# A linear-attention block and a ReLU block: contiguous loads of x, 70 small warming matmuls, the keys' weight on ScalarE's queue, and a new written order

## The chip, the cores and the metric

The kernel runs on 1 core of one Trainium2 chip. The metric is the device time of one execution in microseconds (us), the median of several runs. A core has five engines that work side by side, each on its own list of instructions in order: TensorE (matmuls and weight loads), VectorE, ScalarE, GpSimd and SyncE, which here only issues DMAs. They wait for each other by semaphores.

## The reference

The input x has S = 2048 rows of D = 512 numbers in bfloat16; H = 32 heads of 16; Dff = 1792.

```python
def _A_ref(x, wqkv, wo):          # x is already layer-normed
    qkv = (x @ wqkv) ...          # q, k, v: heads of 16
    phi = lambda t: jnp.where(t > 0, t + 1, jnp.exp(t)) + 1e-6
    pq, pk = phi(q), phi(k)
    kv = jnp.einsum("bhsd,bhse->bhde", pk, v)
    z = jnp.einsum("bhsd->bhd", pk)
    num = jnp.einsum("bhqd,bhde->bhqe", pq, kv)
    den = jnp.einsum("bhqd,bhd->bhq", pq, z)[..., None] + 1e-6
    return (num / den) ... @ wo
def _B_ref(x, w1, w2):
    return relu(x @ w1) @ w2
h = x + _A_ref(_layernorm(x), A_wqkv, A_wo)
return h + _B_ref(_layernorm(h), B_w1, B_w2)
```

The sums over all rows (kv and z) have to be finished before the first row of the attention's output can be made.

## The kernel before

x lies in 16 tiles of 128 rows. Before, row 16 p + t is row p of tile t (`x_v`), so that one tile's rows lie 16 KB apart in memory; the output uses the same order (`of_v`). Tiles are grouped in four chunks of four, 512 columns once they are transposed.

The order of all work is written out by hand in the string `ORDER`. A word such as `K.4.0` calls `op_K(4, 0)`. The words are gone through once, and each engine gets its instructions in the order in which the words issue them; only data, the reuse of a buffer and the reuse of one of eight DMA semaphores make an engine wait. Moving a word past words of other engines alone changes nothing.

First phase, per tile t of x: `lx` loads (SyncE), `S` and `A` make the statistics (VectorE), `R` makes the reciprocal deviation in two small steps (ScalarE), `N` normalises (VectorE; with two more numbers, some of the four 128-column blocks). The normalised tile is then transposed into `lnT`: tiles 0 to 5 by `T` on TensorE, four 128-column matmuls, and a copy out of PSUM by `E` (ScalarE) or `V` (VectorE); tiles 6 to 15 by a DMA transpose, `X`. `K` multiplies a tile's `lnT` by the keys' weight wk (four 512-column matmuls); phi is made of `F` and `U` (ScalarE: exp and relu) and `M` and `D` (VectorE); `G` adds the tile's share of the 512 x 512 product of normalised x and phi(k) to four PSUM banks (four matmuls, bank 4 to 7). After the last tile, `z` sums phi(k) over the rows, `gA`/`gD` copy G out, and `kv`, `kx`, `m` make one matrix of wv and wo that stands for the attention. `Q`, `qF`, `qU`, `qM`, `qD` make phi(q), chunk by chunk.

Second phase, per chunk: `d4`, `dl4`, `dx4` make the reciprocal of den. It is spread over the partitions by `rp` and `rm` for chunk 0 and by a round through memory (`wb`, eight `rb`, `dm`) for the others. Per tile `h` (four matmuls) and `hD` give h; `s`, `a`, `n`, `r` are its layer norm; `t` with `e`/`v` (chunk 0) or `x` (a DMA transpose, chunks 1 to 3) transpose it. `p` is one 128-column block of the product with w1 (four matmuls), `pA`/`pD` its ReLU out of PSUM, `f` the product with w2 (14 matmuls a tile), `fo` the last addition, `fd` the store of a tile. PSUM has eight banks; the last index of `K`, `Q`, `p` and others names the bank.

`lk`, `lq`, `lv`, `lo`, `l1`, `l2` load the weights, all from SyncE. `warm` runs matmuls on zeros, with no reader.

Of the kernel before, what the change touches and what calls it, by code (L numbers as in the profile page):

```python
# [15 lines left out]


ORDER = """
table const masks warm.9.7 lx.1.1 S.1 lx.0.1 S.0 A.0 A.1 lx.2.2 R.1.1 R.0.1 S.3 S.2 A.3 A.2 N.0.0.2 N.0.2.2
N.1 lk.0.2 lx.4.2 lk.2.2 lx.6.2 T.0.0.0.2 warm.1.7 T.0.3.2.2 T.1.1 R.2.2 N.2 T.2.2 E.0.0.2 E.0.2.2 K.0.0 N.3  # L20
S.4 S.5 A.4 A.5 T.3.3 E.1 E.2 F.0.1 K.1.1 U.0.1 R.4.2 F.1.1 V.3 U.1.1 K.3.3 K.2.2 S.6 M.0.1 S.7 D.0.1 N.4 A.6
A.7 M.1.1 N.5 G.0 T.4.0 lo.2.2 lx.8.4 lx.12.4 D.1.1 T.5.1 G.1 R.6.2 F.2.1 E.4 E.5 U.2.1 N.6 S.9 S.8 M.2.1 N.7
A.9 A.8 D.2.1 F.3.1 R.8.2 U.3.1 S.11 M.3.1 X.6 K.4.0 K.5.1 X.7 F.4.2 U.4.2 N.9 D.3.1 S.10 M.4.2 N.8 A.11 D.4.2
A.10 R.10.2 G.2 K.6.2 G.3 K.7.3 F.6.2 U.6.2 S.12 S.13 N.10 A.12 N.11 M.6.2 A.13 X.9 X.8 lq.0.2 lq.2.2 X.10
X.11 D.6.2 R.12.2 G.4 G.5 K.9.1 K.8.0 F.8.2 U.8.2 G.6 G.7 K.10.2 K.11.3 F.10.2 S.14 N.12 N.13 M.8.2 A.14 S.15
D.8.2 A.15 M.10.2 U.10.2 R.14.2 D.10.2 N.14 N.15 X.12 G.8 K.12.0 X.13 X.14 X.15 lv.0.2 l1.0.2 lo.0.2 lv.2.2
l2.0.7 l1.2.2 l2.7.7 K.13.1 U.12.2 F.12.2 M.12.2 G.9 G.10 G.11 Q.0.1.1 Q.0.0.0 K.14.2 K.15.3 qF.0.0.2 qU.0.0.2
F.14.2 U.14.2 D.12.2 G.12 Q.0.3.1 Q.0.2.0 G.13 qM.0.0.2 qD.0.0.2 M.14.2 D.14.2 G.14 z.3.2 z.0.2 z.1.2 z.2.2
qF.0.2.2 qM.0.2.2 zc G.15 gD.0.2 qU.0.2.2 gA.2.2 qD.0.2.2 Q.1.1.3 Q.1.0.2 qU.1.0.2 qF.1.0.2 kv.3.4 kv.0.4
kv.1.4 kv.2.4 kx zh Q.1.3.1 m.0.4 m.1.5 d4.0.3 m.2.6 m.3.7 Q.1.2.0 mD.0.2 dl4.0 dx4.0 qF.1.2.2 qU.1.2.2  # L30
Q.2.1.3 mD.2.2 qM.1.0.2 rp.0.0.4 rp.0.3.7 rp.0.2.6 rp.0.1.5 qM.1.2.2 rm.0.0.2 rm.0.2.2 qD.1.2.2 qD.1.0.2
Q.2.0.2 Q.2.3.1 Q.2.2.0 h.0.4 h.2.6 h.3.7 h.1.5 hD.0 s.0 a.0 n.0 t.0.4 qU.2.0.2 qF.2.0.2 qU.2.2.2 qF.2.2.2 e.0
Q.3.0.2 d4.1.4 hD.2 hD.1 s.2 s.1 hD.3 a.1 a.2 s.3 n.2 a.3 n.1 n.3 Q.3.1.3 Q.3.2.0 Q.3.3.1 t.2.6 t.1.5 t.3.7
dl4.1 dx4.1 qF.3.0.2 qU.3.0.2 e.2 v.1 v.3 wb.1 p.0.0.2 p.0.1.3 rb.1.4 rb.1.2 rb.1.6 rb.1.0 rb.1.5 rb.1.3
rb.1.1 rb.1.7 qF.3.2.2 pD.0.0.2 qU.3.2.2 p.0.2.0 p.0.3.1 p.0.4.2 p.0.5.3 pD.0.4.2 dm.1.0.2 pA.0.2.2 dm.1.2.2
qM.2.2.2 p.0.7.1 p.0.6.0 p.0.8.2 qM.3.2.2 qM.2.0.2 h.7.7 pA.0.6.2 hD.7 h.4.4 hD.4 s.4 qD.3.2.2 h.5.5 h.6.6 a.4
hD.6 hD.5 s.5 s.6 a.6 qM.3.0.2 p.0.11.1 p.0.10.0 a.5 n.6 s.7 qD.2.0.2 a.7 pA.0.10.2 n.4 n.5 p.0.9.3 pA.0.8.2
f.1.5.0.7 p.0.13.3 p.0.12.2 n.7 pA.0.12.2 r.0.4 f.0.4.0.7 f.0.4.7.7 f.3.7.0.7 qD.2.2.2 fo.0 qD.3.0.2 d4.2.4
x.6 x.4 x.5 x.7 f.2.6.0.7 p.1.0.0 p.1.2.2 p.1.3.3 f.3.7.7.7 p.1.1.1 f.1.5.7.7 pD.1.0.2 dl4.2 dx4.2 wb.2 fd.0
rb.2.0 rb.2.4 rb.2.6 rb.2.2 rb.2.1 rb.2.5 rb.2.3 rb.2.7 pA.1.2.2 dm.2.0.2 p.1.6.2 p.1.7.3 dm.2.2.2 pA.1.6.2  # L40
p.1.4.0 p.1.5.1 pA.1.4.2 r.4.4 f.2.6.7.7 fo.3 h.11.7 h.8.4 fo.2 hD.11 fo.1 hD.8 s.11 a.11 s.8 p.1.11.3 p.1.8.0
h.9.5 a.8 hD.9 s.9 a.9 p.1.9.1 h.10.6 hD.10 s.10 a.10 n.8 n.10 p.1.10.2 pD.1.10.2 n.9 pA.1.8.2 p.1.13.1
p.1.12.0 pA.1.12.2 f.4.4.0.7 f.4.4.7.7 n.11 fo.4 fd.1 x.9 fd.3 x.10 x.8 x.11 f.5.5.0.7 d4.3.4 f.7.7.0.7
f.6.6.0.7 f.6.6.7.7 p.2.3.3 dl4.3 r.8.4 dx4.3 p.2.0.0 p.2.2.2 p.2.1.1 f.7.7.7.7 pA.2.0.2 wb.3 rb.3.6 fd.2
rb.3.0 rb.3.4 rb.3.2 rb.3.1 rb.3.5 rb.3.3 rb.3.7 fo.7 fo.6 fd.6 fd.7 p.2.4.0 p.2.5.1 f.5.5.7.7 pA.2.4.2
dm.3.2.2 dm.3.0.2 pA.2.2.2 fo.5 p.2.9.1 h.12.4 h.14.6 h.15.7 h.13.5 p.2.8.0 hD.15 hD.14 hD.12 pA.2.8.2 p.2.7.3
p.2.6.2 p.2.13.1 pA.2.6.2 s.14 hD.13 s.13 a.13 s.12 a.14 s.15 a.15 n.14 a.12 f.8.4.0.7 p.2.10.2 f.9.5.0.7
p.2.11.3 p.2.12.0 n.15 n.12 n.13 pD.2.10.2 f.10.6.0.7 x.13 x.14 x.12 x.15 fd.5 fd.4 r.12.4 pA.2.12.2 f.9.5.7.7
f.10.6.7.7 p.3.1.1 p.3.2.2 p.3.0.0 p.3.3.3 f.8.4.7.7 fo.8 pA.3.0.2 f.11.7.0.7 fo.9 pA.3.2.2 p.3.6.2 p.3.7.3
pA.3.6.2 p.3.5.1 p.3.4.0 p.3.10.2 p.3.11.3 pA.3.4.2 p.3.8.0 p.3.9.1 f.11.7.7.7 pA.3.8.2 fo.11 fo.10 fd.10  # L50
f.12.4.0.7 p.3.13.1 p.3.12.0 f.13.5.0.7 pD.3.10.2 pA.3.12.2 f.15.7.0.14.0.2 f.14.6.0.7 f.13.5.7.7 f.12.4.7.7
fd.11 fd.9 fd.8 fo.13 fo.15.0.2 fo.12 fd.12 fd.15.0.2 fd.13 f.14.6.7.7 fo.14 fd.14 f.15.4.0.14.2.1 fo.15.2.1
fd.15.2.1 f.15.5.0.14.3.1 fo.15.3.1 fd.15.3.1
"""


# [1 line left out]
def kernel(  # L58
# [10 lines left out]
    nc = tc.nc  # L69
    P = 128  # L70
    xf = A_x.flatten_outer_dims()
    of = out.flatten_outer_dims()
    S, D = xf.shape
# [4 lines left out]
    CW = 512  # L78
# [7 lines left out]
    NO = 4  # L86

    const = ctx.enter_context(tc.tile_pool(name="const", bufs=1))
# [3 lines left out]

    ctx.enter_context(tc.manual_schedule())

    x_v = xf.rearrange("(p t) d -> p t d", p=P)
    of_v = of.rearrange("(p t) d -> p t d", p=P)
    wqkv_v = A_wqkv.rearrange("(k p) n -> p k n", p=P)
    wo_v = A_wo.rearrange("(k p) n -> p k n", p=P)
    w1_v = B_w1.rearrange("(k p) n -> p k n", p=P)
# [2 lines left out]
    x_nat = big.tile([P, NT, D], BF16, name="x_nat")  # L102
    wq_sb = const.tile([P, KD, D], BF16, name="wq_sb")
    wk_sb = const.tile([P, KD, D], BF16, name="wk_sb")
# [30 lines left out]
    rb = big.tile([P, NE, 2, CW], BF16, name="rb")  # L135
# [6 lines left out]
    o_t = gT  # L142
    zeros = m_sb[:, 0, :]
    bk = psum.tile([P, 8, CW], F32, name="bk")
# [52 lines left out]


    def op_lx(t, n):
        nc.sync.dma_start(out=x_nat[:, t : t + n, :], in_=x_v[:, t : t + n, :])  # L200

    def load_d(dst, src, k, n):
        nc.sync.dma_start(out=dst[:, k : k + n, :], in_=src[:, k : k + n, :])

    op_lk = lambda k, n: load_d(wk_sb, wqkv_v[:, :, D : 2 * D], k, n)
    op_lq = lambda k, n: load_d(wq_sb, wqkv_v[:, :, 0:D], k, n)
    op_lv = lambda k, n: load_d(wv_sb, wqkv_v[:, :, 2 * D : 3 * D], k, n)
    op_lo = lambda k, n: load_d(wo_sb, wo_v, k, n)
    op_l1 = lambda k, n: load_d(w1_sb, w1_v, k, n)
    op_l2 = lambda k, n: load_d(w2_sb, w2_v, k, n)  # L210

    def op_warm(n, b):
        for _ in range(n):
            nc.tensor.matmul(bk[:, b, :], lhsT=zeros[:, 0:P], rhs=zeros, start=True, stop=True)


    op_S = lambda t: nc.vector.bn_stats(out=st[:, t, :], in_=x_nat[:, t, :])  # L217
# [271 lines left out]

    def op_fd(t, k=0, w=KD):  # L490
        cols = slice(k * P, (k + w) * P)
        nc.sync.dma_start(out=of_v[:, t, cols], in_=o_t[:, t % NO, cols])

    ops = {k[3:]: v for k, v in locals().items() if k.startswith("op_")}
    for word in ORDER.split():
# [32 lines left out]
```

## Time and profile before

| | |
|---|---|
| median of 3 runs | 175.04 us (173.61, 175.04, 175.33) |
| profiled execution | 175.75 us, of which the span is 174.0 us |
| TensorE busy | 165.3 us, 870 matmuls |
| VectorE, ScalarE, GpSimd busy | 90.3, 69.9, 4.7 us |
| first DMA issue | 0.80 us |
| last output issue | 171.62 us |
| HBM read, written | 9.44 MB, 2.49 MB |

The span runs from the first to the last instruction of the profiled execution; the device time of the same execution is 1.75 us longer. A matmul's length in the profile includes its way through the array, so matmuls overlap; what they cost is the distance between their starts. A line of the timeline has start, length, engine, line of the source, operation, out<-in, shape and count, and in brackets the idle time of the engine before it and what ended that. In the profile's DMA lists "to landing" is the time from an issue on SyncE to the arrival of the last of its 16 completions.

### The profile page before, as it was taken

Reading aid. Unit: us, or ns where it says so; the run is one execution under the profiler, and the core shown is the slowest. Engines: PE = TensorE matmul, PEld = TensorE weight load, DVE = VectorE, ACT = ScalarE, POOL = GpSimd, SP = SyncE. Lnnn points to the kernel's source line nnn. Section 1 sums busy time; section 2 is a strip of 40 time slices with the busy share of each in tenths; the row PEclk is TensorE's granted clock in tenths of the full one; section 3 lists DMA queues with packets and bytes.
Section 4 is the critical chain, followed back from the end, with each engine's and each line's share of the span. In section 5 each row is a group of like instructions: output and inputs, shape, how many; then the busy total and the mean of one; then the engine's idle time right before and its main releaser. Section 6 shows DMA issues by size and latency. Waiting matters only on the chain.

```text
span 174.0 us, 2293 instructions
## 1 busy us (share of the span) xinstructions
PE 165.3 (95%) x870; PEld 77.5 (45%) x886; DVE 90.3 (52%) x194; ACT 69.9 (40%) x102; POOL 4.7 (3%) x21
## 2 busy tenths in 40 slices
PE   7499989999999989999999999999999999999993
PEld 2255434446534444444444444444444444444643
DVE  3779975532689935995305597101659201205043
ACT  2488756675678582243321322302414204241100
POOL 7300000000000000000000000000000000000000
PEclk9999999999999999999999999999999999999999
DMA  4951454289900032004131000555200430002104
GB/s 123 317 223 30 90 157 90 49 276 363 375 25 2 0 101 53 0 0 86 38 120 61 0 30 2 122 65 145 66 0 0 90 94 0 0 0 86 34 4 121
DMA packets 22475, 14.97 MB, mean 86 GB/s; under 512 B 13248, under 2 KB 21312, under 8 KB 22464
## 3 DMA queue, kind: packets, MB, share of 16 engines
q1 hardware_dynamic: 22464, 14.82, 29.9%
q8 instruction: 7, 0.11, 0.3%
q14 instruction: 4, 0.03, 0.1%
HBM read 9.44 MB, written 2.49 MB: 69 GB/s over the span
## 4 chain that ended last, share of the span: by engine, by line
PE 85%; DVE 5%; DMA 5%; issue 1%; ACT 1%; SPq 0%
PE bk L448 28%; PE bk L477 28%; PE bk L433 8%; PE bk L287 8%; PE bk L331 5%; PE bk L279 4%; DMA lnT<-h_nat 3%; DMA x_nat<-in_A_x_dram 2%; DVE st L217 2%; PE bk L250 1%; PE bk L339 1%; PE bk L386 1%; PE bk L373 1%; DVE h_nat L231 1%; ACT eb L297 1%
## 5 line engine op out<-in xcount | busy, mean ns | idle before, releaser
L448 PE MATMUL bk<-lnT,w_sb 128*128 128x512 bf16 x223 | 51.1, 379 | 0.8 <-DVE lnT L269 0.7
L477 PE MATMUL bk<-w_sb,at 128*128 128x512 bf16 (+2 forms) x244 | 50.3, 355 | 0.4
L463 ACT ACTIVATE at<-bk 128x1024 bf16<-128x1024 f32 x22 | 22.2, 1023 | 62.0 <-PE bk L448 56.8
L477 PEld LDWEIGHTS <-at 128*128 128x128 bf16 x252 | 23.4, 98 | 25.1 <-issue 0.5
L485 DVE SCALAR_TENSOR_TENSOR gT<-bk,rstd,h_nat 128x512 bf16<-128x512 f32 (+2 forms) x18 | 12.1, 688 | 43.0 <-PE bk L477 42.8
L448 PEld LDWEIGHTS <-w_sb 128*128 128x128 bf16 x224 | 21.8, 98 | 27.3 <-issue 0.9
L297 ACT ACTIVATE eb<-bk 128x1024 bf16<-128x1024 f32 (+1 forms) x18 | 16.7, 927 | 7.2 <-PE bk L279 4.2
L300 ACT ACTIVATE rb<-bk 128x1024 bf16<-128x1024 f32 (+1 forms) x18 | 16.7, 928 | 1.2 <-PE bk L287 1.0
L279 PE MATMUL bk<-wk_sb,lnT 128*128 128x512 bf16 x64 | 16.1, 390 | 0.8 <-DMA lnT<-h_nat 0.7
L287 PE MATMUL bk<-lnT,wq_sb 128*128 128x512 bf16 x62 | 14.9, 379 | 0.2 <-issue 0.2
L433 PE MATMUL bk<-m_sb,pqs 128*128 128x512 bf16 x63 | 14.6, 379 | 0.1
L468 DVE TENSOR_SCALAR at<-bk 128x1024 bf16<-128x1024 f32 x6 | 7.3, 1222 | 13.9 <-PE bk L448 13.9
L331 PE MATMUL bk<-at,h_nat 128*128 128x512 bf16 x53 | 13.1, 379 | 0.1
L439 DVE TENSOR_TENSOR h_nat<-bk,x_nat 128x512 bf16<-128x512 f32 x16 | 10.6, 681 | 3.1 <-PE bk L433 2.9
L217 DVE BATCH_NORM_STATS2 st<-x_nat 128x6 f32<-128x512 bf16 x16 | 10.5, 680 | 3.0 <-DMA x_nat<-in_A_x_dram 3.0
L304 DVE TENSOR_SCALAR eb<-eb 128x1024 bf16<-128x1024 bf16 (+1 forms) x18 | 6.8, 387 | 7.9 <-ACT eb L297 7.8
L219 DVE BATCH_NORM_STATS2 st<-h_nat 128x6 f32<-128x512 bf16 x16 | 10.7, 680 | 0.2
L279 PEld LDWEIGHTS <-lnT 128*128 128x128 bf16 x64 | 6.3, 101 | 8.4 <-DMA lnT<-h_nat 1.2
L433 PEld LDWEIGHTS <-pqs 128*128 128x128 bf16 x64 | 6.2, 98 | 7.6
L331 PEld LDWEIGHTS <-h_nat 128*128 128x128 bf16 x64 | 6.1, 98 | 7.1
L287 PEld LDWEIGHTS <-wq_sb 128*128 128x128 bf16 x64 | 6.0, 98 | 7.1 <-issue 0.5
L223 ACT ACTIVATE rstd<-mv,eps 128x2 f32<-128x2 f32 (+2 forms) x13 | 3.8, 293 | 7.0 <-DVE mv L218 5.7
(58 smaller groups left out, 84.8 us busy)
## 6 DMA issues: line engine op xcount, KB each, us to landing
w_sb<-in_B_w_dram SPq DMA_DIRECT2D x4, 896.0 KB, 9.6
out_dram<-gT SPq DMA_DIRECT2D x15, 128.0 KB, 1.9
rr<-scr SPq DMA_DIRECT2D x24, 64.0 KB, 2.7
x_nat<-in_A_x_dram SPq DMA_DIRECT2D x2, 512.0 KB, 7.3
x_nat<-in_A_x_dram SPq DMA_DIRECT2D x3, 256.0 KB, 4.5
wk_sb<-in_A_wqkv_dram SPq DMA_DIRECT2D x2, 256.0 KB, 4.4
wo_sb<-in_A_wo_dram SPq DMA_DIRECT2D x2, 256.0 KB, 5.3
wq_sb<-in_A_wqkv_dram SPq DMA_DIRECT2D x2, 256.0 KB, 4.1
```

Source lines behind the costliest of these rows:

```text
L217: op_S = lambda t: nc.vector.bn_stats(out=st[:, t, :], in_=x_nat[:, t, :])
L219: op_s = lambda t: nc.vector.bn_stats(out=st2[:, t, :], in_=h_nat[:, t, :])
L279: nc.tensor.matmul(bk[:, b, :], lhsT=lnT[c][:, kd, j * P : (j + 1) * P], rhs=wk_sb[:, kd, :], start=(kd == 0), stop=(kd == KD - 1),)
L287: nc.tensor.matmul(bk[:, b, :], lhsT=wq_sb[:, kd, j * P : (j + 1) * P], rhs=lnT[c][:, kd, :], start=(kd == 0), stop=(kd == KD - 1),)
L297: nc.scalar.activation(out=buf(eb, kind, i, n), in_=bank(at_bank[kind, i], n), func=ACT.Exp)
L300: nc.scalar.activation(out=buf(rb, kind, i, n), in_=bank(at_bank[kind, i], n), func=ACT.Relu)
L331: nc.tensor.matmul(bk[:, KD + kd, :], lhsT=ln_nat[:, t, kd * P : (kd + 1) * P], rhs=pk(t)[:, 0, :], start=(t == 0), stop=(t == NT - 1),)
L433: nc.tensor.matmul(bk[:, b, :], lhsT=pqs[:, (c * KD + jb) % NQ, j * P : (j + 1) * P], rhs=m_sb[:, jb, :], start=(jb == 0), stop=(jb == KD ...
L448: nc.tensor.matmul(bk[:, b, :], lhsT=w1_sb[:, kd, f * P : (f + 1) * P], rhs=lnT[c][:, kd, :], start=(kd == 0), stop=(kd == KD - 1),)
L463: nc.scalar.activation(out=acts[c % 2][:, f : f + n, :], in_=bank(at_bank["p", c, f], n), func=ACT.Relu)
L477: nc.tensor.matmul(bk[:, b, 0 : w * P], lhsT=acts[c % 2][:, f, j * P : (j + 1) * P], rhs=w2_sb[:, f, k * P : (k + w) * P], start=(f == 0), ...
L485: nc.vector.scalar_tensor_tensor(out=o_t[:, t % NO, cols], in0=bk[:, at_bank["f", t, k], 0 : w * P], scalar=rstd2[:, t : t + 1], in1=h_nat ...
```

## The change

- Rows of x and of the output are assigned to tiles by `GROUPS`: a group of n tiles is n x 128 rows that follow each other in memory, and partition p has n of them. Tiles 0 to 3 are groups of one.
- x's first four tiles are loaded one by one, in the order 1, 2, 0, 3, then 4-5, 6-7, 8-11, 12-15, with no weight between them on SyncE's queue. Before: 1, 0, 2-3, then 4-5, 6-7, 8-11, 12-15 with wk and half of wo between them.
- wk's two halves are issued by ScalarE (`lkA`), behind its table load.
- The first warming is 70 matmuls of 64 columns in place of 9 of 512. The second, one of 512 columns, stands ahead of all transposes; it stood between tile 0's halves.
- The other words are in a new order. The same tiles are transposed by TensorE and by DMA as before, and the matmuls beside the warming are the same in number and shape.

The core of the diff; of `ORDER`, the words up to the first of the w1 matmuls:

```diff
-table const masks warm.9.7 lx.1.1 S.1 lx.0.1 S.0 A.0 A.1 lx.2.2 R.1.1 R.0.1 S.3 S.2 A.3 A.2 N.0.0.2 N.0.2.2
-N.1 lk.0.2 lx.4.2 lk.2.2 lx.6.2 T.0.0.0.2 warm.1.7 T.0.3.2.2 T.1.1 R.2.2 N.2 T.2.2 E.0.0.2 E.0.2.2 K.0.0 N.3
-S.4 S.5 A.4 A.5 T.3.3 E.1 E.2 F.0.1 K.1.1 U.0.1 R.4.2 F.1.1 V.3 U.1.1 K.3.3 K.2.2 S.6 M.0.1 S.7 D.0.1 N.4 A.6
-A.7 M.1.1 N.5 G.0 T.4.0 lo.2.2 lx.8.4 lx.12.4 D.1.1 T.5.1 G.1 R.6.2 F.2.1 E.4 E.5 U.2.1 N.6 S.9 S.8 M.2.1 N.7
-A.9 A.8 D.2.1 F.3.1 R.8.2 U.3.1 S.11 M.3.1 X.6 K.4.0 K.5.1 X.7 F.4.2 U.4.2 N.9 D.3.1 S.10 M.4.2 N.8 A.11 D.4.2
-A.10 R.10.2 G.2 K.6.2 G.3 K.7.3 F.6.2 U.6.2 S.12 S.13 N.10 A.12 N.11 M.6.2 A.13 X.9 X.8 lq.0.2 lq.2.2 X.10
-X.11 D.6.2 R.12.2 G.4 G.5 K.9.1 K.8.0 F.8.2 U.8.2 G.6 G.7 K.10.2 K.11.3 F.10.2 S.14 N.12 N.13 M.8.2 A.14 S.15
-D.8.2 A.15 M.10.2 U.10.2 R.14.2 D.10.2 N.14 N.15 X.12 G.8 K.12.0 X.13 X.14 X.15 lv.0.2 l1.0.2 lo.0.2 lv.2.2
-l2.0.7 l1.2.2 l2.7.7 K.13.1 U.12.2 F.12.2 M.12.2 G.9 G.10 G.11 Q.0.1.1 Q.0.0.0 K.14.2 K.15.3 qF.0.0.2 qU.0.0.2
...
-Q.3.0.2 d4.1.4 hD.2 hD.1 s.2 s.1 hD.3 a.1 a.2 s.3 n.2 a.3 n.1 n.3 Q.3.1.3 Q.3.2.0 Q.3.3.1 t.2.6 t.1.5 t.3.7
-dl4.1 dx4.1 qF.3.0.2 qU.3.0.2 e.2 v.1 v.3 wb.1 p.0.0.2 p.0.1.3 rb.1.4 rb.1.2 rb.1.6 rb.1.0 rb.1.5 rb.1.3
+table const masks warm.70.7.64 lx.1.1 S.1 lx.2.1 S.2 lx.0.1 lx.3.1 lx.4.2 lx.6.2 lkA.0.2 S.0 A.1 lkA.2.2 R.1.1
+lx.8.4 A.2 A.0 S.3 N.1 A.3 R.0.1 R.2.2 N.0.0.2 N.0.2.2 S.5 N.3 warm.1.7 T.0.3.2.2 T.0.0.0.2 E.0.2.2 T.1.1
+E.0.0.2 E.1 T.3.3 N.2 E.3 T.2.2 S.6 S.4 A.5 A.4 A.6 S.7 A.7 E.2 R.4.2 N.4 K.0.0 F.0.1 M.0.1 N.5 U.0.1 R.6.2
+D.0.1 K.1.1 K.3.3 F.1.1 N.7 N.6 M.1.1 T.4.0 K.2.2 G.0 S.9 S.8 U.1.1 E.4 D.1.1 A.8 T.5.1 U.2.1 F.2.1 E.5 A.9
+M.2.1 R.8.2 F.3.1 U.3.1 S.10 D.2.1 K.4.0 G.1 lx.12.4 X.7 lq.2.2 X.6 N.8 S.12 S.11 N.9 A.11 A.10 K.5.1 M.3.1
+F.4.2 M.4.2 D.3.1 R.10.2 U.4.2 S.13 N.11 A.13 D.4.2 A.12 G.2 K.7.3 K.6.2 G.3 F.6.2 R.12.2 U.6.2 X.8 lo.2.2 X.9
+X.11 lq.0.2 K.8.0 G.4 K.9.1 F.8.2 U.8.2 N.13 N.12 M.6.2 D.6.2 N.10 S.14 M.8.2 S.15 A.14 A.15 D.8.2 R.14.2 N.14
+N.15 X.13 G.5 K.11.3 G.6 K.13.1 X.12 K.12.0 G.7 X.10 l2.7.7 X.15 X.14 lv.2.2 lv.0.2 l1.0.2 l2.0.7 l1.2.2
+lo.0.2 G.8 K.10.2 F.12.2 U.12.2 F.10.2 U.10.2 Q.0.0.0 Q.0.1.1 G.9 M.10.2 D.10.2 M.12.2 qF.0.0.2 qU.0.0.2
...
+qF.2.0.2 e.0 Q.3.0.2 d4.1.4 hD.3 hD.2 s.3 s.2 hD.1 a.2 a.3 s.1 n.3 a.1 n.2 n.1 Q.3.1.3 Q.3.3.1 Q.3.2.0 t.3.7
+t.2.6 v.3 t.1.5 v.1 dl4.1 dx4.1 wb.1 rb.1.2 rb.1.6 rb.1.0 rb.1.4 rb.1.7 rb.1.1 rb.1.3 rb.1.5 qF.3.0.2 qU.3.0.2
...
-    x_v = xf.rearrange("(p t) d -> p t d", p=P)
-    of_v = of.rearrange("(p t) d -> p t d", p=P)
+    GROUPS = [(0, 1), (1, 1), (2, 1), (3, 1), (4, 2), (6, 2), (8, 4), (12, 4)]
+    group_of = {t: g for g in GROUPS for t in range(g[0], g[0] + g[1])}
+    def rows_of(f, t, n):
+        t0, g = group_of[t]
+        v = f[t0 * P : (t0 + g) * P, :].rearrange("(p t) d -> p t d", t=g)
+        return v[:, t - t0 : t - t0 + n, :]
...
     def op_lx(t, n):
-        nc.sync.dma_start(out=x_nat[:, t : t + n, :], in_=x_v[:, t : t + n, :])
-    def load_d(dst, src, k, n):
-        nc.sync.dma_start(out=dst[:, k : k + n, :], in_=src[:, k : k + n, :])
+        nc.sync.dma_start(out=x_nat[:, t : t + n, :], in_=rows_of(xf, t, n))
+    def load_d(dst, src, k, n, queue=None):
+        (queue or nc.sync).dma_start(out=dst[:, k : k + n, :], in_=src[:, k : k + n, :])
+    op_lkA = lambda k, n: load_d(wk_sb, wqkv_v[:, :, D : 2 * D], k, n, nc.scalar)
...
-    def op_warm(n, b):
+    def op_warm(n, b, w=CW):
         for _ in range(n):
-            nc.tensor.matmul(bk[:, b, :], lhsT=zeros[:, 0:P], rhs=zeros, start=True, stop=True)
+            nc.tensor.matmul(bk[:, b, 0:w], lhsT=zeros[:, 0:P], rhs=zeros[:, 0:w], start=True, stop=True)
...
-        nc.sync.dma_start(out=of_v[:, t, cols], in_=o_t[:, t % NO, cols])
+        nc.sync.dma_start(out=rows_of(of, t, 1)[:, 0, cols], in_=o_t[:, t % NO, cols])
```

## The prediction

> **What bounds the kernel now.** I read the engine shares and slices first, then TensorE's waits, then TensorE and VectorE in order of time, last the chain of work that ended last.
>
> ```profile
> PE 165.3 (95%) x870; PEld 77.5 (45%) x886; DVE 90.3 (52%) x194; ACT 69.9 (40%) x102; POOL 4.7 (3%) x21
> ...
> PE   7499989999999989999999999999999999999993
> ```
>
> TensorE is full from the third slice (8.7 us) to the last. All its waits that have an owner are these:
>
> ```profile
> PE bk L250 <- DVE h_nat L231: 2.3, 1, 2.3
> PE bk L214 <- DVE ones L176: 1.3, 1, 1.3
> PE bk L279 <- DMA lnT<-h_nat: 0.7, 1, 0.7
> PE bk L448 <- DVE lnT L269: 0.7, 1, 0.7
> ```
>
> So a change that leaves TensorE's work alone can act in three places: the start, the wait for a transposed tile, and the step into the w1 matmuls. TensorE in order of time (start, length, line, count):
>
> ```profile
> 1.25 4.02 PE L214 MATMUL bk<-m_sb 128*128 128x512 bf16 x9 [1.25 <-DVE ones L176]
> 7.54 0.39 PE L250 MATMUL bk<-ident,h_nat 128*128 128x128 bf16 x2 [2.26 <-DVE h_nat L231]
> 7.72 0.63 PE L214 MATMUL bk<-m_sb 128*128 128x512 bf16 x1
> 8.15 1.27 PE L250 MATMUL bk<-ident,h_nat 128*128 128x128 bf16 x10
> 9.21 1.63 PE L279 MATMUL bk<-wk_sb,lnT 128*128 128x512 bf16 x4
> ...
> 22.58 1.03 PE L279 MATMUL bk<-wk_sb,lnT 128*128 128x512 bf16 x4
> 24.35 1.04 PE L279 MATMUL bk<-wk_sb,lnT 128*128 128x512 bf16 x4 [0.75 <-DMA lnT<-h_nat]
> ```
>
> Two paces are seen. The nine warming matmuls start every 0.427 us, the ten transposes every 0.107 (1.07 us on the chain), and K.0's four also start 0.427 apart until the third. From about 10.43 us a 512-column matmul starts every 0.216 and a transpose every 0.056; in the trace the record of the full clock begins at 10.43. Before that, TensorE ran at half pace. From 10.43 the stream is dense: what looks like a gap of 0.2 every 64 matmuls is a missing record.
>
> VectorE before the first transpose:
>
> ```profile
> 3.13 1.29 DVE L217 BATCH_NORM_STATS2 st<-x_nat 128x6 f32<-128x512 bf16 x2 [1.91 <-DMA x_nat<-in_A_x_dram]
> 4.45 0.25 DVE L218 BATCH_NORM_AGGREGATE mv<-st 128x2 f32<-128x6 f32 x2
> 5.74 1.29 DVE L217 BATCH_NORM_STATS2 st<-x_nat 128x6 f32<-128x512 bf16 x2 [1.05 <-DMA x_nat<-in_A_x_dram]
> 6.95 0.30 DVE L218 BATCH_NORM_AGGREGATE mv<-st 128x2 f32<-128x6 f32 x2
> 7.16 1.54 DVE L231 TENSOR_SCALAR h_nat<-x_nat,mv,rstd 128x256 bf16<-128x256 bf16 x5
> ```
>
> Tile 0's normalising stands behind the statistics of tiles 2 and 3, and those wait for the third load (issued 1.72, landed 5.72, 4.0 us). The last step, from the chain (start, length, what):
>
> ```profile
> 61.55 0.46 PE bk L250 x8
> 62.01 0.02 issue
> 62.03 0.77 DVE lnT L269 x2
> 62.80 0.14 issue
> 62.93 7.93 PE bk L448 x36
> ```
>
> **The front, part by part.** *Warming.* 70 matmuls of 64 columns take the place of nine of 512. No row shows 64 columns at half pace. Below stands the column sum at L339 (64 pairs of weight load and 1-column matmul in 1.58 us, 25 ns each), above the 128-column transpose at half pace, 107 ns. I take half of 107, 53 ns, since the work per column decides in the second row and a weight load of the same size hides in it: 70 x 0.053 = 3.7 us, so from 1.25 to 5.0. The single 512-column matmul now comes ahead of all transposes: to 5.4. Both lie inside the wait for x, and 0.43 us leaves the path, where it stood between the first transposes. At 107 ns the end is 9.2, which is a rival below; at 25 ns it is 3.4, hidden too.
>
> The Trainium skill speaks against the 53 ns: its page "TensorE: Matmul & The Clock Gate", section "LDWEIGHTS (loading the stationary operand)", gives a weight load as columns / 1.2 ns, which is 107 ns for these 128 columns and 7.5 us for the 70. L339's 25 ns per pair contradicts it in this trace; by the rule the sum would be that of the rival.
>
> *x and wk.* SyncE issues x1, x2, x0, x3 as single tiles (0.46 us apart: 0.80, 1.26, 1.72, 2.19), then 4-5, 6-7, 8-11, 12-15 with no wk between. The first two loads of before took 2.3 and 2.1 us to land; for the new third and fourth I take 2.1 (3.8 and 4.3), the old 4.0 being the upper end (5.7 and 6.2). Packet sizes hardly change (1 KB a row for one tile, 4 KB for four), the addresses become contiguous. wk moves to ScalarE's queue: two issues of 0.43, at the earliest at 0.80 beside the table load (0.80 to 2.08), at the latest after it, when ScalarE has nothing to do until the first rstd. wk is needed at 8.7; before it took 4.3 to 4.6 us, so it lands by 7.1.
>
> *VectorE's new walk*, a statistic being issued every 0.61 and an aggregate every 0.1: S.1 3.13, S.2 3.74, S.0 4.35 (x0 there by 3.8), A.1, A.2, A.0 from 4.95 to 5.3, S.3 5.25, N.1 5.85 (its rstd on ScalarE, 0.53 after the aggregate of 5.1, is ready at 5.7), A.3 6.2, N.0's halves 6.3 and 6.5, done at 6.84. The first transpose starts at 6.9 instead of 7.54. S.5 follows at 6.8, N.3 7.4, N.2 7.7. TensorE: T.0 and T.1 at half pace 6.9 to 7.75, T.3 7.84, T.2 8.26, end 8.7. K.0 starts at 8.7 instead of 9.21, with T.3's 0.22 already done: 0.73 gained. Until 10.43 the pace is half: K.0 ends at 10.4, its excess over 0.86 is 0.85, where before it was 0.60: 0.25 lost. Net **0.5 us**. If the old 4.0 us of landing hold, S.3 moves to 5.7 and the first transpose to 7.4: then 0.25 net.
>
> **The rest of the order.** *The wait at 23.2 to 24.35 us* cost 1.13 - 0.22 = 0.91. X.8's transpose landed 4.4 us after its issue, against a median of 2.5: on two of its 16 completions, at 24.2, while all others were done by 22.3. At 21.76 an instruction fetch of 16 KB took 1.35 us of a DMA engine. Such fetches come seven times, every 250 TensorE instructions or so; the new kernel has 122 more at the start, so each comes about 61 pairs (13 us) earlier, the first near K.0. There the last x loads absorb it: they landed by 12.8, and S.9 reads them at about 13. I count **0.91** as gained. K.8 is then reached at 20.35 with X.8 issued at about 16.2. The new waits near it are short of biting: G.3 (19.5) wants D.3 (19.0), G.4 (21.2) wants D.4 (20.65), K.13 (25.5) wants X.13 (24.8 with lq behind it), K.10 (29) wants X.10 (26.7). These margins of about 0.5 us are the weak point.
>
> *Weights.* wv, w1, w2 and the second half of wo go out after X.14 (about 29.5), one w2 half already before X.15. 3.5 MB at the 288 GB/s that the old group reached (4.46 MB in 34.4 to 50.0) is 12.3 us: 42, wanted by kv and m at 44.3 and 45.2. Hidden; with the cover gone m waits.
>
> *Into w1.* t.3 comes first and VectorE copies it while t.2 and t.1 run; before, both copies (0.77 together) came after t.1. Now one comes early, but the other still waits for t.1, which is now last instead of second (0.22 later): 0.35 less 0.22, **0.1**.
>
> *From 63 us on* TensorE has the same matmuls, and was dense. I followed evacuations, statistics and transposes of each chunk with the rows' durations (h_nat 0.60 issue to issue, statistics 0.60, pair evacuations 1.02 on ScalarE and 1.22 on VectorE): lnT1 is there 1.2 us, lnT2 0.7, lnT3 1.5 before its first matmul. Before, lnT2 had 0.1. I take 0, between a loss of 1 (one fetch on a transpose) and a gain of 0.
>
> *Output in contiguous rows*: only the last 32 KB lie on the path (171.62 to 173.06, 1.44 us; the page has 1.5, 1.7 and 1.9 for 32, 64, 128 KB). The packets stay 256 B: 0, within 0.3 either way.
>
> **Sum.** 0.5 + 0.9 + 0.1 = 1.5 us. The profiled execution took 175.75: 174.0 of span and 1.75 around it, giving 172.5 and 174.25. It lies 0.7 above the median of the runs (175.04), so against the median: **173.5 us**. Its own range is 172.9 to 174.5, from the x landing (+0.25), the margins (+0.5) and the fetches.
>
> **Rivals.** *Full pace early, 172.4.* The three runs are 173.61, 175.04, 175.33. Half pace cost before 12 x 0.051 + 0.21 + 0.60 = 1.4 us, near that spread, so one of the three may have been at full pace by the first transpose. With warming to 5.4 and work from 6.9, the idle stretch shrinks from 2.5 to 1.5 us, which speaks for it; the profiled execution speaks against it. K.0 then ends at 9.25 instead of 10.4, 1.1 less. The Trainium skill's page "TensorE: Matmul & The Clock Gate", section "What's actually happening", has the clock gate judged in a free-running window of 3.4 us, so that the moment varies from run to run; no row here shows the window.
>
> *A wait in another place, 174.4.* The margins above are half a microsecond; one transposed tile hit by a fetch or by the 0.9 MB of w2 that now follow X.10 costs again 0.91. For it: X.8's 4.4 us. Against: the fetches' shift.
>
> *Weight load visible, 174.6.* 107 ns a pair: warming ends at 9.2, the transposes at 10.66, K.0 at 11.5, 1.1 behind the forecast. Only the 25 ns of L339 speak against.
>
> *wk ahead of x, slower: 176.5.* If ScalarE's issue at 0.80 isn't held by the table load, 512 KB of wk share the engines with x0 and x3: at the 324 GB/s of 7.0 to 10.4 us, 1.6 us. The first transpose moves to 8.5 and the idle stretch to 3.1, longer than before's 2.5, and it decides from there: the warming then counts for nothing, and full pace comes no earlier than 3.8 us after 8.5 (so long did the nine run without it) and at worst 9.2 after (1.25 to 10.43). K.0 starts at 10.2; at 12.3 TensorE is 1.7 behind the forecast, at 17.7 4.4 behind: 175.2 to 177.9. Against: x1 and x2 are issued early, and a fair share costs x0 and x3 less than all of it. The Trainium skill's "DMA: Bandwidth & Descriptors", section "Issuing engines are not separate DMA queues", says that both queues run on the same 16 engines and interleave; the trace has one queue and can't show it.
>
> **Numbers.** Forecast 0.36, early pace 0.25, wait elsewhere 0.14, wk ahead 0.17, weight load 0.08. Faster by over 1% means below 173.3 (1% is about what a measurement of this kernel can tell from no change): the early pace, nearly half of the forecast (0.17), and 0.06 of others: 0.48. Slower by over 1%, above 176.8: half of wk ahead and 0.06 for chains that I followed wrongly: 0.15. The range 172.0 to 176.0 leaves out the end of the wk case and little else.
>
> **What would show it.** First transpose at 6.9 (right) or 7.5 and later (x late); warming pairs 53 ns apart; no TensorE wait on a transposed tile near 23 us; kv at 44.4 instead of 45.98; the w1 matmuls starting at about 61.4; TensorE dense from there. Wrong it is with a first transpose after 8, half pace past 11 us, or a new wait over 1 us between 12 and 45 us.

## The result and the profile after

The changed kernel takes 175.5 us (median of 20 runs, 174.77 to 176.8) where the kernel before takes 174.84 us on the same chip (median of 20, 173.29 to 175.58): a ratio of 1.0058, 95% interval 1.0033 to 1.0083. It is slower, by 0.6%; 173.5 was forecast. The 175.5 us lie inside the stated range of 172.0 to 176.0, but on the other side of before than was forecast. A ratio compares the runs within 1.5% of the fastest of their kernel, so it isn't the ratio of the medians shown; it leaves out most in e5, three of twelve, and of the runs left out one of before and one of e10 had a granted clock of 0.86.

The two profiled executions stand the other way round. That of after took 175.06 us (span 173.3), 0.4 under its median; that of before took 175.75 us, slower than every one of the 20 runs of before just named. What follows compares the two traces by their places in time, and takes the sizes from the experiments, with both the ratio and the traces where they differ.

The page of after, its TensorE row and the granted clock in 40 slices (PEclk counts the time ahead of the first record, at 4.40, as full pace; the distances of the matmuls show half pace there):

```profile
PE 165.7 (96%) x947; PEld 79.9 (46%) x947; DVE 95.0 (55%) x197; ACT 66.3 (38%) x99; POOL 4.7 (3%) x21
...
PEclk9979999999999999999999999999999999999999
```

TensorE's waits. The first line was 2.3 us before. The wait for `lnT` by DMA (0.7 before) is not in the list any more:

```profile
PE bk L258 <- DVE h_nat L239: 3.0, 1, 3.0
PE bk L222 <- DVE ones L183: 1.3, 1, 1.3
PE bk L456 <- DVE lnT L277: 0.6, 1, 0.6
```

TensorE in order of time:

```profile
1.25 3.84 PE L222 MATMUL bk<-m_sb 128*128 128x64 bf16 x71 [1.25 <-DVE ones L183]
8.06 1.95 PE L258 MATMUL bk<-ident,h_nat 128*128 128x128 bf16 x16 [2.97 <-DVE h_nat L239]
9.81 3.46 PE L287 MATMUL bk<-wk_sb,lnT 128*128 128x512 bf16 x12
...
23.04 1.03 PE L287 MATMUL bk<-wk_sb,lnT 128*128 128x512 bf16 x4
23.91 1.03 PE L339 MATMUL bk<-at,h_nat 128*128 128x512 bf16 x4
...
62.37 1.89 PE L456 MATMUL bk<-lnT,w_sb 128*128 128x512 bf16 x8 [0.61 <-DVE lnT L277]
```

The small warming matmuls do end at 5 us, and where before had a hole from 23.2 to 24.35 the stream is dense. But the first transpose stands at 8.06, not earlier than before's 7.54 but later, and K.0 at 9.81 (before 9.21). The w1 matmuls start at 62.37 (before 62.93), and from there both kernels need the same: 108.0 us to the last matmul's start (before 108.05).

What the first transpose waits for is seen on VectorE. Each of the first three statistics waits for its own load:

```profile
2.98 0.69 DVE L225 BATCH_NORM_STATS2 st<-x_nat 128x6 f32<-128x512 bf16 x1 [1.76 <-DMA x_nat<-in_A_x_dram]
4.18 0.69 DVE L225 BATCH_NORM_STATS2 st<-x_nat 128x6 f32<-128x512 bf16 x1 [0.51 <-DMA x_nat<-in_A_x_dram]
5.61 0.69 DVE L225 BATCH_NORM_STATS2 st<-x_nat 128x6 f32<-128x512 bf16 x1 [0.74 <-DMA x_nat<-in_A_x_dram]
```

In the trace x1, x2, x0, x3 land at 2.95, 4.16, 5.59 and 6.21, that is 2.1, 2.9, 3.9 and 4.0 us after their issues. ScalarE shows what went out beside them (ACTq is the part of ScalarE that issues DMAs):

```profile
0.79 1.28 ACT L172 ACT_TABLE_LOAD   x1 [0.79 <-PEq L520]
0.82 0.97 ACTq L210 DMA_DIRECT2D wk_sb<-in_A_wqkv_dram  x2
```

wk's two halves go out at 0.82 and 1.30 us, in the middle of the table load and not behind it, the first ahead of x2 (1.25), the second ahead of x0 and x3 (1.72 and 2.19). 512 KB of wk travel beside the 512 KB of x's first four tiles. That this is the cause is what e1 and e2 test.

The pace, in three windows (TensorE's busy time and count; PEclk is the granted clock):

```profile
4.40:7.80 3.40, 0.69 (x16) 0.38 (x13) 2.66 (x10) 1.15 (x5) 1.45 (x6) 1.00 1.02 364
7.80:11.22 3.42, 3.15 (x20) 2.19 (x21) 3.42 (x10) 2.93 (x9) 0.00 (x0) 0.50 0.45 181
11.22:14.00 2.78, 2.78 (x18) 1.35 (x17) 2.36 (x10) 2.40 (x8) 0.00 (x0) 1.00 0.00 0
```

Full pace is granted at 4.40, near the end of the warming (its pairs go from 53 to 29 ns). Then TensorE idles for 3.0 us, and at 7.81, just ahead of the first transpose, it is taken away again, for 3.41 us. All sixteen transposes run 107 ns apart, and K.0 427.

### The profile page after: what moved, and what is told of

Same layout as the page of the kernel before. It is cut to its first block, busy times and chain, and to the rows that moved or that the text cites. A ratio compares the mean times of both kernels' runs of the same rounds, so it can differ in the third digit from the quotient of the medians.

```text
span 173.3 us, 2433 instructions
## 1 busy us (share of the span) xinstructions
PE 165.7 (96%) x947; PEld 79.9 (46%) x947; DVE 95.0 (55%) x197; ACT 66.3 (38%) x99; POOL 4.7 (3%) x21
## 4 chain that ended last, share of the span: by engine, by line
PE 93%; DMA 2%; DVE 2%; SPq 0%; issue 0%
PE bk L485 28%; PE bk L456 28%; PE bk L287 8%; PE bk L295 8%; PE bk L339 8%; PE bk L441 8%; DMA x_nat<-in_A_x_dram 2%; PE bk L258 2%; PE bk L347 1%; DVE st L225 1%; PE bk L394 1%; PE bk L381 1%; PE bk L369 1%; DVE lnT L277 0%; SPq L207 0%; DVE h_nat L239 0%
## 5 line engine op out<-in xcount | busy, mean ns | idle before, releaser
L471 ACT ACTIVATE at<-bk 128x1024 bf16<-128x1024 f32 x18 | 18.4, 1022 | 64.3 <-PE bk L456 64.3
L476 DVE TENSOR_SCALAR at<-bk 128x1024 bf16<-128x1024 f32 x10 | 12.2, 1224 | 20.8 <-PE bk L456 20.7
L339 PE MATMUL bk<-at,h_nat 128*128 128x512 bf16 x56 | 13.7, 379 | 0.0
L227 DVE BATCH_NORM_STATS2 st<-h_nat 128x6 f32<-128x512 bf16 x16 | 10.6, 684 | 0.2
L432 DVE TENSOR_TENSOR pqs<-pqT,rr 128x1024 bf16<-128x1024 bf16 x6 | 4.0, 686 | 7.1 <-DMA rr<-scr 7.1
```

The lines of the kernel that those rows point to most:

```text
L339: nc.tensor.matmul(bk[:, KD + kd, :], lhsT=ln_nat[:, t, kd * P : (kd + 1) * P], rhs=pk(t)[:, 0, :], start=(t == 0), stop=(t == NT - 1),)
L471: nc.scalar.activation(out=acts[c % 2][:, f : f + n, :], in_=bank(at_bank["p", c, f], n), func=ACT.Relu)
L476: nc.vector.tensor_scalar(out=acts[c % 2][:, f : f + n, :], in0=bank(at_bank["p", c, f], n), scalar1=0.0, scalar2=None, op0=ALU.max,)
```

## The experiments

Three things were to be told apart: (1) wk beside x makes x late; (2) the warming ends too long before the transposes, so that the pace granted early is lost again; (3) the 70 extra pairs move an instruction fetch away from tile 8's transpose and gain there. The expectations name their theories anew each time. Each ratio is taken against runs of the kernel before on the same chip; e11 is a single execution.

**e1: wk back on SyncE.** In the changed kernel's order:

```diff
-lx.3.1 lx.4.2 lx.6.2 lkA.0.2 S.0 A.1 lkA.2.2 R.1.1
+lx.3.1 lk.0.2 lx.4.2 lk.2.2 lx.6.2 S.0 A.1 R.1.1
```

> The changed kernel with wk's two halves issued by SyncE again, one after x's first four tiles and one after tiles 4-5; the rest unchanged. Theory 1 (wk beside x): x2, x0 and x3 came late because 512 KB of wk shared the DMA engines with them, so without it x0 lands by 4.3 us and x3 by 4.9 (in the changed kernel 5.6 and 6.2), the first transpose starts at 6.9 to 7.2 instead of 8.06, and the time falls by 1.0 to 2.5 us under the changed kernel's 175.5: 173.0 to 174.5, faster than before. Rival (layout): the single contiguous 128 KB loads themselves are slow; then x0 still lands after 5.2, and the time stays within 0.4 of 175.5.

174.66 us, ratio 0.9973 (0.9936 to 1.0009). x0 and x3 land at 3.94 and 4.48, 2.2 and 2.3 us after their issues, and TensorE shows:

```profile
6.61 0.62 PE L258 MATMUL bk<-ident,h_nat 128*128 128x128 bf16 x8 [1.84 <-DVE h_nat L239]
```

The first transpose comes 1.45 us earlier than in after, by the move of two DMA issues alone. Against after's ratio of 1.0058 that is some 0.85%, 1.5 us; the medians differ by 0.84, and in the two traces the w1 matmuls start 0.83 earlier (61.54). On e1's own chip, e4 below, which is after but for the row layout, took 1.5 us more than e1. The pace is lost here as well (granted 4.17, lost 7.58, back at 11.0).

**e2: the same step alone, in the kernel before.**

```diff
-warm.9.7 lx.1.1 S.1 lx.0.1 S.0 A.0 A.1 ... N.1 lk.0.2 lx.4.2 lk.2.2 lx.6.2
+warm.9.7 lx.1.1 S.1 lx.0.1 lkA.0.2 lkA.2.2 S.0 A.0 A.1 ... N.1 lx.4.2 lx.6.2
```

> The kernel before, with wk alone moved to ScalarE's queue ahead of all its other work. Theory 1: x0 and x2-3 land later (3.4 and 5.7 us before; now about 4.2 and 6.5), the first transpose moves from 7.54 to 8.2 or later, and the kernel is 0.5 to 1.8 us slower than before. Rival (order or layout is the cause): moving wk costs nothing in this kernel, within 0.3 of before.

176.75 us, ratio 1.0084 (1.0057 to 1.011): 1.5 us lost. x0 lands at 4.69 and tiles 2 and 3 at 6.39 (before: 5.72 for the latter).

```profile
8.20 0.40 PE L251 MATMUL bk<-ident,h_nat 128*128 128x128 bf16 x2 [3.48 <-DVE h_nat L232]
...
24.79 1.04 PE L280 MATMUL bk<-wk_sb,lnT 128*128 128x512 bf16 x4 [0.63 <-DMA lnT<-h_nat]
```

The first line is the late start again, the second the wait for tile 8, still there. (1) is shown from both sides.

**e3: 130 warming matmuls of 64 columns in after**, to bridge the idle time.

```diff
-table const masks warm.70.7.64
+table const masks warm.130.7.64
```

> The changed kernel with 130 warming matmuls of 64 columns instead of 70, so that TensorE is busy until about 6.5 us (full pace granted near 4.4) or 8.2 us (not granted). Theory 2 (pace): the changed kernel was granted full pace at 4.4 us and lost it at 7.8 because TensorE idled for 3.1 us; with the idle stretch at 1.6 us or less the pace is kept, 16 transposes take 0.9 instead of 1.7 us and K.0 0.86 instead of 1.57; the first transpose stays at 8.1. Time 1.0 to 1.5 us under the changed kernel: 174.0 to 174.5. Rival (VectorE and ScalarE set the pace there anyway): the transposes are faster but T.4, G.0 or K.4 then wait, and the time stays within 0.4 of 175.5.

175.94 us, ratio 1.0042 (1.0011 to 1.0073); the expected time was missed. The pace half came true: full pace is granted at 4.67 and kept, the transposes run 56 ns apart, and K.0 starts at 9.45. But further down stands

```profile
26.28 1.90 PE L287 MATMUL bk<-wk_sb,lnT 128*128 128x512 bf16 x7 [0.56 <-DMA lnT<-h_nat]
```

a loss of 0.72 us that after hasn't. With 120 more instructions the 16 KB fetches lie at 9.03 and 22.55 instead of 10.39 and 38.81: the second fell among the DMA transposes, as before's at 21.76 did.

**e4: the old row layout in after.**

```diff
-        v = f[t0 * P : (t0 + g) * P, :].rearrange("(p t) d -> p t d", t=g)
-        return v[:, t - t0 : t - t0 + n, :]
+        return f.rearrange("(p t) d -> p t d", p=P)[:, t : t + n, :]
```

> The changed kernel with the rows of x and of the output assigned as before (row 16 p + t), the loads and stores otherwise as in the changed kernel. Theory 1: landing times of x within 0.3 us of the changed kernel's (2.95, 4.16, 5.59, 6.21), time within 0.4 of 175.5: the layout does nothing measurable. Rival A (contiguous helps): x lands later still, time 0.5 to 1.5 us longer. Rival B (contiguous hurts): x0 and x3 land earlier, time 0.7 us or more shorter.

176.18 us, ratio 1.0043 (1.0014 to 1.0073), against after's 1.0058 (1.0033 to 1.0083): the contiguous rows make no difference that was measured. x0 and x3 land at 5.88 and 6.20 (after 5.59 and 6.21). This profiled execution had full pace only from 13.67 us. Its 176.44 us are the length of after's five longest runs (176.3 to 176.8), and their mean granted clock is like its own (0.998 to 0.999; after's other runs 0.99). That those five also got full pace late is likely and not shown.

**e5: 70 matmuls of 64 columns in the kernel before**, alone (with the width as a third argument of the helper, as in the change).

```diff
-table const masks warm.9.7
+table const masks warm.70.7.64
```

> The kernel before with its nine warming matmuls of 512 columns replaced by 70 of 64 columns, nothing else. They take as long (3.7 us), but add 122 instructions to TensorE's list. Theory 3 (fetch): the wait for X.8's tile at 23 us comes from a 16 KB instruction fetch on a DMA engine; 122 more instructions move the fetch from 21.8 us to about 9 to 11, X.8 lands 2.5 us after its issue, TensorE doesn't wait near 23 us, and the kernel is 0.5 to 1.0 us faster than before. Rival (the two wq loads issued behind X.8 share the engines with it): the wait stays, and the time is within 0.3 of before.

174.83 us, ratio 0.9945 (0.9905 to 0.9986). The first fetches are at 10.63 and 38.78, and K.8, which waited before, runs on:

```profile
22.76 1.89 PE L279 MATMUL bk<-wk_sb,lnT 128*128 128x512 bf16 x8
```

The pace is lost from 8.48 to 11.90. So what the small matmuls bring here is (3), by their number: 1 us by the ratio, 0.6 by the medians (before 175.45).

**e6: e1 with 70 matmuls of 96 columns.**

```diff
-warm.70.7.64
+warm.70.7.96
```

> The changed kernel with wk on SyncE's queue as in the first experiment, and the 70 warming matmuls 96 columns wide instead of 64, so that they end between 5.7 and 6.9 us with the same number of instructions. Theory 2 (pace): TensorE idles less than 1.2 us before the first transpose at 6.6 to 7.0, full pace is never lost, and the time falls another 0.7 to 1.2 us under that experiment's 0.9973 of before: 0.990 to 0.993 of before. Rival (VectorE and ScalarE bound the first 14 us anyway): within 0.3 us of that experiment.

174.33 us, ratio 0.9943 (0.9915 to 0.9972). Full pace comes at 4.34 (the pairs go from 80 to 42 ns) and isn't lost. The gain over e1, 0.3% (0.5 us), is less than expected: TensorE now outruns the others. Its list of waits has two new lines, the first ahead of tile 3's transposes (1.05 us lost), the second ahead of tile 4's (0.74):

```profile
PE bk L258 <- ACT lnT L268: 0.9, 1, 0.9
...
PE bk L258 <- ACT rb L308: 0.6, 1, 0.6
```

For tile 3 the named copy and the normalising on VectorE end within 0.1 us of each other (8.26 and 8.2, the transpose starts at 8.29); e12 asks which it is. For tile 4 the owner is `U.0`, which reads bank 0 until 12.13 and holds it against `T.4`; it stands on ScalarE behind the reciprocal deviation of tiles 4 and 5, and that behind VectorE's statistics.

**e7: after with 70 matmuls of 128 columns**, wk left on ScalarE.

```diff
-warm.70.7.64
+warm.70.7.128
```

> The changed kernel with its 70 warming matmuls 128 columns wide, wk still on ScalarE's queue: TensorE is busy until 6.9 us or later, with no more instructions than the changed kernel has (the run with 130 matmuls moved a fetch onto a transposed tile and lost 0.7 us there). Theory 2: x lands as late as in the changed kernel, the first transpose starts at 8.0 to 8.3, but at full pace; 0.9 to 1.4 us under the changed kernel, 0.998 to 1.001 of before. Rival: within 0.3 us of the changed kernel, 1.004 to 1.008 of before.

174.24 us, ratio 0.9942 (0.9915 to 0.9969). The fetches stay where after has them (10.28, 37.66), the first transpose stays late (7.96), and only the pace differs:

```profile
1.25 5.65 PE L222 MATMUL bk<-m_sb 128*128 128x128 bf16 x70 [1.25 <-DVE ones L183]
7.96 0.62 PE L258 MATMUL bk<-ident,h_nat 128*128 128x128 bf16 x8 [1.06 <-DVE h_nat L239]
```

By the ratios that is 1.2% under after, 2.0 us, more than the forecast of this run; by the medians it is 1.26, and in the two traces the w1 matmuls start 0.96 earlier. The ratios go further because the median of before was 174.84 in the runs beside after and 175.45 in those beside e7. Eleven of e7's twelve runs lie between 174.12 and 174.69. (2) holds: warming to 5 us was too short for an x that comes at 8.

**e8: 14 warming matmuls of 512 columns in the kernel before** (9 there). Few instructions more, so the fetches hardly move.

```diff
-table const masks warm.9.7
+table const masks warm.14.7
```

> The kernel before with 14 warming matmuls of 512 columns instead of 9, which fill the wait for x (to 5.8 us where full pace is granted near 4, to 7.3 where it isn't). Theory 2: the idle stretch before the first transpose falls from 2.5 to under 1.8 us, fewer runs lose full pace or get it late, and the median falls by 0.7 to 1.4 us, 0.992 to 0.996 of before. Rival: pace at the start is hidden behind VectorE, and the median stays within 0.3 us of before.

174.39 us, ratio 0.9956 (0.9928 to 0.9985). Full pace is kept, and the runs lie between 174.2 and 175.12 where before's spread from 173.86 to 177.05 on this chip. Full pace comes at 4.20. The fetch is at 20.56, and the wait for tile 8 is there (0.95 us lost). (2) and (3) are separate terms.

**e9: both in the kernel before**, 70 matmuls of 128 columns.

```diff
-table const masks warm.9.7
+table const masks warm.70.7.128
```

> The kernel before with its first warming as 70 matmuls of 128 columns; queues, layout and order stay. Theory 1 (an instruction fetch strikes tile 8's DMA transpose): as many TensorE instructions are added as in e5, so the first fetch comes near 10.5 us and the wait near 23 us is absent: 0.9 us gained. Theory 2 (the pace): the warming ends near 7, the first transposes follow within 0.6 us, full pace is kept. Both gains together: about 173.2 us where before runs at 175.4, a ratio of 0.985 to 0.990, below e5 (0.9945, fetch alone) and e8 (0.9956, pace alone). Rival: the two gains aren't additive, because what VectorE has ready after tile 3 (tiles 4 and 5) is late for a TensorE that runs faster, as in e6: then 0.992 to 0.995 and a TensorE wait of 0.5 to 1 us between 10 and 14 us.

173.35 us, all twelve runs between 173.0 and 173.89; ratio 0.9924 (0.9892 to 0.9955). It beats both kernels and has the lowest median of all that were run, 1.0 us under e8, which keeps the pace and has the wait for tile 8. Full pace comes late here, at 7.1 by the distances of the matmuls, but the warming reaches to the first transpose (7.93). The first line shows it; the other two are all the waits that TensorE has left in the whole span:

```profile
1.25 6.85 PE L214 MATMUL bk<-m_sb 128*128 128x128 bf16 x70 [1.25 <-DVE ones L176]
...
PE bk L214 <- DVE ones L176: 1.2, 1, 1.2
PE bk L448 <- DVE lnT L269: 0.7, 1, 0.7
```

The median fell as expected, while the ratio is above the expected band: the runs of before that it is taken against have a median of 174.8 here, where 175.4 was expected. The rival's wait between 10 and 14 us is absent.

**e10: e1 with 70 matmuls of 128 columns.**

```diff
-warm.70.7.64
+warm.70.7.128
```

> The changed kernel with wk issued by SyncE behind x's first four loads (as in e1) and the first warming as 70 matmuls of 128 columns (as in e7). The warming ends near 7 and x's first four tiles land by 4.5, so the first transpose starts near 7.1 to 7.3 at full pace, where e7 had 7.96. If the start of the transposes were what counts, 0.7 to 0.8 us under e7's 174.24: 173.5 (ratio 0.990). If the next thing is late, as e6 showed for tile 4's transposes (0.74 us of wait at 12), nearly nothing is gained over e7: 174.1 to 174.4 (0.993 to 0.995), with a wait of 0.6 to 0.9 us near 12 us.

174.35 us, ratio 0.9985 (0.9949 to 1.0021). In its trace the granted clock is 0.85 from 7.18 us on, so only the start is read:

```profile
1.25 7.23 PE L222 MATMUL bk<-m_sb 128*128 128x128 bf16 x71 [1.25 <-DVE ones L183]
8.31 1.40 PE L258 MATMUL bk<-ident,h_nat 128*128 128x128 bf16 x16
```

By time the second expectation holds: most runs lie at 174.1 to 174.6, as e7's do. Its sign, a wait near 12 us, isn't in this trace. Here the warming itself held the first transpose until 8.31, later than e7's 7.96, so x's earlier landing could gain nothing. Whether that is so in the other runs isn't shown. Against e9 on the same chip, the old order with the same warming, e10 is 0.6% behind by the ratios, and only one of its runs (173.66) is as short as any of e9's.

**e11: the kernel before once more**, for a second profile.

> The kernel before, unchanged, for a second profile. Asked is which parts of its first profile repeat. Theory 1: the fetch near 21.8 us and the wait of about 0.9 us for tile 8's transpose are there again, as the fetches go by the count of TensorE's instructions. Theory 2: the pace may differ: an execution near 174 us has full pace before 8 us, one near 175 to 176 has half pace until about 10 to 11. Rival: the wait for tile 8 is an accident of the one execution and is absent here.

175.25 us, span 173.5. The fetch is at 21.31, the wait for tile 8 is there too, with 0.50 lost instead of 0.91. The start is another: tiles 2 and 3 land at 5.02 instead of 5.72, the first transpose is at 6.83, full pace is granted at 4.81, lost at 8.22 and back at 11.64. So the wait repeats, and half pace until 11.64 does too, but by an early grant that is lost and not by one late grant. The w1 matmuls start at 62.35, after's 62.37.

**e12: e6 with two pairs of words exchanged on VectorE.**

```diff
-S.5 N.3 warm.1.7 ... S.6 S.4 A.5 A.4 A.6 S.7
+N.3 S.5 warm.1.7 ... S.4 A.5 A.4 S.6 A.6 S.7
```

> e6 with two pairs of words exchanged on VectorE, nothing else: N.3 ahead of S.5, and S.4 A.5 A.4 ahead of S.6. Theory (the new order's statistics stand in an order written for an x with no weight between its loads; with wk back on SyncE's queue tile 3's normalising waits behind the load of tiles 4-5 and tile 4's behind that of 6-7): TensorE's waits of 1.0 us ahead of tile 3's transposes and of 0.6 us ahead of tile 4's shrink to under 0.3 each, K.0 starts near 8.3 where e6 had 8.85, and the time falls from e6's 174.3 to 173.0 to 173.4, the time of e9 (ratio 0.988 to 0.992). Rival: phi of tile 0, made on ScalarE and VectorE behind the same statistics, is late next, and G.0 waits for it: 173.8 to 174.3 and a new TensorE wait of 0.5 us or more between 11 and 14 us.

173.93 us, ratio 0.9933 (0.99 to 0.9967), against e6's 0.9943: not told apart. The expected 173.0 to 173.4 was missed; the time is in the rival's band. K.0 starts at 8.31 as expected. The loss ahead of tile 3 shrinks from 1.05 to 0.30, so it was VectorE's; 0.44 comes up ahead of tile 2, whose normalising now stands behind tile 5's statistics. That ahead of tile 4 stays, 0.61 of 0.74:

```profile
11.61 0.40 PE L258 MATMUL bk<-ident,h_nat 128*128 128x128 bf16 x4 [0.45 <-ACT rstd L231]
```

Bank 0 is free by 10.6 now, and VectorE is last: it normalises tile 4 (11.17 to 11.55) only behind both statistics of tiles 6 and 7, whose load landed at 9.53. So the theory holds for tile 3 and missed tile 4. The rival had the size of the wait, but its place, G.0, isn't where the time goes.

## Why the prediction was wrong

**The x and wk term failed, first by its place.** The text took 2.1 us of landing for x0 and x3 and gave wk's issue no cost. Measured were 3.9 and 4.0 us, with wk out at 0.82. This was written down as the rival "wk ahead of x", at 0.17, and it is what happened: it expected the first transpose at 8.5 (8.06 seen), an idle stretch of 3.1 us (3.0 seen) and 175.2 to 177.9 us. It was put low on the words that x1 and x2 are issued early; wk's first half was out before x2. The deciding question, whether ScalarE's queue issues during the table load, was stated and not answered; no row of before could answer it. By their ratios e1 and e2 give 1.5 us for it, by the traces of after and e1 it is 0.8. The text did have a case for landings of 4.0 us, with the first transpose at 7.4 and a net gain of 0.25, but its own walk doesn't give that. From S.0 to the first transpose the walk counts 2.55 us (4.35 to 6.9); with x0 at 5.7 that makes 8.25. Measured were S.0 at 5.61 and the first transpose at 8.06. The Trainium skill's page "DMA: Bandwidth & Descriptors", section "Issuing engines are not separate DMA queues", which the prediction cited in that rival, says that DMAs of all issuing engines run on the same 16 DMA engines and interleave. The runs agree: with wk on the second queue x0 and x3 landed 3.9 and 4.0 us after their issues, without it 2.2 and 2.3 (e1).

**The pace followed, as a rival's step and not as the forecast's.** Half pace lasted to 11.22, past the 11 us that the text named as its own refutation. What it hadn't seen is that full pace is granted before 5 us and then lost: it reckoned with one late grant (10.43 in before's profile). e7 and e8 show this term alone (0.96 us in e7's trace). The Trainium skill's page "TensorE: Matmul & The Clock Gate", section "What's actually happening", has a window of 3.4 us; the record of after shows two such stretches, 4.40 to 7.81 and 7.81 to 11.22.

**The base was wrong for a comparison of medians.** The sum of 1.5 us was made on an execution slower than all of the 20 runs of before that stand against after, and was then taken off the median. Of the 2.0 us between forecast and median, 0.8 lie in the traced execution (175.06, where 174.25 was forecast for it), 0.4 between it and after's median, and 0.75 in the step from 174.25 to 173.5. e11 shows what was particular to it: x2 and x3 0.7 later, and 0.4 more at tile 8. Traced against the first profile of before the change gains 0.56 at the w1 matmuls; against the second it gains nothing (62.37 and 62.35).

**The wait at 23 us was right** in its mechanism: fetches by the count of instructions, 0.91 gone (e5; e2, e8 and e11 still have the wait, e3 has it back at another tile). The size was that of one execution; e11 lost 0.50.

**Right in the rest.** The warming pair takes 53 ns until full pace, then 29. The 53 was half of a neighbouring row, but its reason holds too: at half pace pairs of 96 columns take 80 ns (e6) and of 128 columns 107 (e7), so the time goes by the columns of the matmul and the weight load hides. The estimate of 107 ns for each weight load, worked out from the Trainium skill's page "TensorE: Matmul & The Clock Gate", section "LDWEIGHTS (loading the stationary operand)", isn't seen at 64 columns. The step into w1 lost 0.77 instead of 0.88, as forecast 0.1. No weight is waited for, and after 63 us nothing changes. K.0 ends at 11.37 where 10.4 was forecast, 0.97 behind. kv (45.53 on the chain) and the w1 matmuls (62.37) are 1.1 and 1.0 behind their marks, so between K.0 and the w1 matmuls hardly anything is left unexplained.

By ratios, from before to after in three steps: the small matmuls -0.55% (e5), the new order with the contiguous rows +0.28% (e5 to e1), wk on ScalarE +0.85% (e1 to after; 0.84% in e2, which is measured on its own). The second step's intervals overlap widely, so by itself it isn't shown. With the pace kept it is larger, 0.6% in e10 against e9, whose intervals just overlap (0.9949 and 0.9955). Which words cost it is open beyond tile 4's place in VectorE's queue (e6, e12).

## What to carry to other kernels

A load that is moved to an idle engine's queue can go out earlier, and here what it then took from the loads that the first work needs counted for more than the issue time saved: check when that queue is first free before calling it hidden. Warming matmuls have to reach close to the first real ones, so size them by when the data lands: here an early grant was kept with 1.6 us of idle time or less ahead of the first transpose, and lost with 1.7 or more. e9 reached the first transpose and, by the number of its matmuls, also moved a fetch out of the way. Before a sum is set against a median, look whether the profiled execution is a typical one of the runs.

## What the runs showed of the hardware

- A DMA on ScalarE's queue is issued while its table load runs (0.82 and 1.30 us in a load from 0.79 to 2.08).
- Where an early grant of full pace was lost, it lasted 3.41 us, and half pace another 3.41 (after, e1, e2, e5, e11). The grant came between 4.0 and 5.1 us in ten traces, and later in three (before 10.43, e4 13.67, e9 7.1), which nothing here explains. Worked out from the distances of the matmuls, TensorE was busy for about 15 to 36% of the 3.41 us behind the early grant where the pace was then lost, and for about 50 to 70% where it was kept (e3, e6, e7, e8, e12). The idle time ahead of the first transpose parts the same traces (1.73 to 3.48 us lost, 0.31 to 1.55 kept); which of the two decides isn't shown.
- The 16 KB instruction fetches come with the count of TensorE's instructions. When one came at 20.6 to 22.6 us, among the DMA transposes, TensorE waited (0.50 to 0.95 us in before, e2, e3, e8, e11); with 61 more pairs it came at 10.3 to 11.0 and the wait was gone (after, e1, e5, e6, e7, e9, e12).
